# Linear attention with an adapter mixture on one core: one store for a slot, split first loads, values loaded at fixed steps, k passes on ScalarE

## The chip, the cores and the metric

The program runs on one core of a Trainium2 chip. The core has five engines with their own instruction streams, which wait for one another through semaphores: TensorE (PE, with its weight loads shown as PEld), VectorE (DVE), ScalarE (ACT), GpSimd (POOL) and SyncE (SP). SP does no arithmetic here; it issues transfers between HBM and SBUF. Sixteen transfer engines carry them out. The metric is the time of one execution on the device, in microseconds (us); the median of three runs is shown.

## What is computed

An attention with a linear kernel (eight batches, eight heads, 576 positions, 64 features), and behind it a mixture of low-rank adapters of which each row takes two out of eight:

```python
def phi(x, c, s):
    r = np.maximum(x, 0.0)
    return np.concatenate([r * c, r * s], axis=-1)    # c, s: cos, sin of pi/2 * pos/S
q_p = phi(q, cos_w, sin_w)
k_p = phi(k, cos_w, sin_w)
kv = np.einsum('bhsf,bhsd->bhfd', k_p, v)
z = np.sum(k_p, axis=2)
num = np.einsum('bhsf,bhfd->bhsd', q_p, kv)
den = np.einsum('bhsf,bhf->bhs', q_p, z)[..., None] + 1e-06
x = (num / den)                       # then (batch, position) x (head, feature): 4608 x 512
logits = x @ w_gate                   # 8 experts
topk = two largest of logits, w = softmax over these two
out = x + sum over the two of w_k * (x @ A[e]) @ B[e]     # rank 16
```

Inputs and the output are float32; the matrix products run in bf16 with float32 sums.

## The kernel before

**Layout.** A batch's 576 positions are 64 rows of nine neighbours: position 9p + i is row p, column i. Two halves of the heads are stacked, so a tile of k, q or v has 128 partitions (64 rows, twice) and four heads x nine columns x 64 features in each: 1,152 KB in float32. An output tile ("slot", 0 to 35) holds two columns: 128 rows of the output, 64 for each column, 512 values each. Nine slots make a pair of batches; the fifth slot of a pair takes its second column from the second batch.

**Per batch.** `load_k`, `load_q` (SP's queue) and `load_v` (POOL's queue, which also turns v into bf16) bring a batch in. `scale_k(u)` makes relu(k) times cos and sin for one column u of one batch, `kv(u)` multiplies it with v and adds up in PSUM over nine columns, with a column of ones for z. `kv_out` copies the sum to SBUF.

**Per slot n.** `scale_q` (POOL) multiplies two columns of q by cos and sin, four instructions for a slot; `transp_q` (PE) turns them, `evac_q` (DVE) copies them out with the relu; `numden` (PE) makes numerator and denominator; `normalise` (DVE: reciprocal and product) gives the row block xt; `transp_x` (PE) and `evac_x` (DVE) turn it; `logits` (PE) makes x A and x w_gate in one product. Gates are made for groups of three slots (the last slots are groups of two and one): `gate_max`, `gate_a`, `gate_sig` (ACT's sigmoid), `gate_em`, `gate_b`, then `transp_z` and `evac_z` (zgT). `delta` (PE) adds x and z B in PSUM, `evac_o` (ACT, or DVE) copies the sum to SBUF, `store` writes it out.

**Order.** The order on each engine is written out by hand; no scheduler moves anything. The loop runs over n from 0 to 34. In step n the kernel normalises slot n, makes `numden` for n + 1, turns q for n + 2 and scales q for n + 3. `kv_at[n]` lists the columns of k that enter kv in step n; their `scale_k` stands one step earlier. In step n, `age` holds how many steps ago a group's last slot was normalised: at 1 comes `gate_max`, at 2 sigmoid, `gate_em`, `gate_b` and `transp_z`, at 3 `evac_z`; from then on one `delta`, `evac_o` and `store` in each step. Slot d is stored in step d + 5. Behind the loop the last six slots are written out one by one.

**Waits that matter here.** The tile `xz` is one PSUM bank that holds the turned x (columns 0 to 511), the turned z (512 to 895) and a zero that the DVE form of the sin pass reads (line 153). Waits are kept for the tile as a whole: `transp_x` waits for a sin pass on DVE that stands before it, and for `evac_z`. SP and POOL issue in order. Each transfer of SP uses one of eight semaphores in turn and waits until the transfer eight issues earlier has landed. A result tile has 14 buffers (`p_o`), a scaled column of k eight (`p_kp`), v four.

**Start.** SP issues k, v, q of batch 0, k, q of batch 1, then A, w_gate and B, then k, q of batch 2. 32 matmuls on zeros warm PE up. v of batch 0 comes in float32 and is turned into bf16 by DVE and POOL; POOL issues v of batch 1 and 2 before the loop, 3 and 4 in steps 0 and 1 (`load_at`), together with k and q.

Of the kernel before, what the change touches and what calls it, by code (L numbers as in the profile page):

```python
# [18 lines left out]
HALF = 64  # L19
NC = 9  # L20
# [5 lines left out]
def kernel(ctx, tc, q, k, v, w_gate, A, Bw, out):  # L26
# [15 lines left out]
    p_q = ctx.enter_context(tc.tile_pool(name="p_q", bufs=4))  # L42
    p_kp = ctx.enter_context(tc.tile_pool(name="p_kp", bufs=8))
    p_qp = ctx.enter_context(tc.tile_pool(name="p_qp", bufs=3))
# [17 lines left out]

    def part(dram, b):

        a = dram[b, 0:1, 0:1, 0:1]
        return bass.AP(a.tensor, a.offset, [[NC * D, 128], [2 * S * D, HP], [1, NC * D]])

    def load_k(b):
        k_t[b] = p_k.tile([128, HP, NC, D], FP32, name="ks")
        nc.sync.dma_start(out=k_t[b].rearrange("p j i d -> p j (i d)"), in_=part(k, b))  # L70

    def load_q(b):
        q_t[b] = p_q.tile([128, HP, NC, D], FP32, name="qs")
        nc.sync.dma_start(out=q_t[b].rearrange("p j i d -> p j (i d)"), in_=part(q, b))  # L74

# [4 lines left out]

    load_k(0)
    v0 = p_k.tile([128, HP, NC, D], FP32, name="ks")
    nc.sync.dma_start(out=v0.rearrange("p j i d -> p j (i d)"), in_=part(v, 0))
    load_q(0)
    load_k(1)
    load_q(1)

# [41 lines left out]
    Ball = persist.tile([128, DM], BF16, name="Ball")  # L129
    load_k(2)  # L130
    load_q(2)

# [9 lines left out]
    def scale_k(u):  # L142

        b, i = divmod(u, NC)
        kp_t[u] = kp = p_kp.tile([128, HP, 2, D], BF16, name="kp")
        src = k_t[b][:, :, i, :]
        nc.scalar.activation(kp[:, :, 0, :], src, AF.Relu, bias=0.0, scale=cos_tab[:, i:i + 1])  # L147
        if b == 0:
            nc.vector.tensor_scalar(out=kp[:, :, 1, :], in0=src, scalar1=sin_tab[:, i:i + 1],
                                    scalar2=0.0, op0=ALU.mult, op1=ALU.max)  # L150
        elif i % 4 == 3 or (b == 1 and i % 2):

            nc.vector.scalar_tensor_tensor(out=kp[:, :, 1, :], in0=src,  # L153
                                           scalar=sin_tab[:, i:i + 1],
                                           in1=zero.to_broadcast([128, HP, D]),
                                           op0=ALU.mult, op1=ALU.max)
        else:
            nc.scalar.activation(kp[:, :, 1, :], src, AF.Relu, bias=0.0,  # L158
                                 scale=sin_tab[:, i:i + 1])
# [90 lines left out]
    for g, tiles in enumerate(groups):  # L250
        for n in tiles:
            free = groups[g - 1][-1] + 3 if 0 < g < len(groups) - 1 else 0
            due.setdefault(max(n + 1, free, 3), []).append(n)

    def logits(n):
        g = group_of[n]
        i = n - groups[g][0]
        if i == 0:
            za_t[g] = ps.tile([128, 3, ZW], FP32, name="za",
                              tag="qpTp" if g == len(groups) - 1 else "za")  # L260
        xT = xT_t.pop(n)
# [5 lines left out]

    far = set(range(len(groups) - 2))

    def gate_max(g):  # L270
        G = len(groups[g])
        l = za_t[g][:, 0:G, ER:ZW]
        if g in far:
            src = l
            l = p_g.tile([128, 3, 8], FP32, name="lg")
            nc.vector.tensor_scalar(out=l[:, 0:G], in0=src, scalar1=2.0, scalar2=None,
                                    op0=ALU.mult)
            l = l[:, 0:G]
        m8 = p_g.tile([128, 3, 8], FP32, name="m8")
        for i in range(G):  # L280
# [3 lines left out]
                                in1=m8[:, 0:G, 1].to_broadcast([128, G, 8]), op=ALU.is_ge)  # L284
        g_t[g] = (l, m8, mask)

    def gate_a(g):
        G = len(groups[g])
        l, m8, mask = g_t[g]
        nm = p_g.tile([128, 3], FP32, name="nm")  # L290
        t = p_g.tile([128, 3, 8], FP32, name="tg")
        if g in far:
            nc.gpsimd.tensor_tensor(out=nm[:, 0:G], in0=m8[:, 0:G, 0], in1=m8[:, 0:G, 1],  # L293
                                    op=ALU.add)
            nc.gpsimd.tensor_tensor(out=t[:, 0:G], in0=l,
                                    in1=nm[:, 0:G].to_broadcast([128, G, 8]), op=ALU.subtract)
        else:
            nc.vector.scalar_tensor_tensor(out=nm[:, 0:G], in0=m8[:, 0:G, 0], scalar=-1.0,
                                           in1=m8[:, 0:G, 1], op0=ALU.mult, op1=ALU.subtract)
            nc.vector.scalar_tensor_tensor(out=t[:, 0:G], in0=l, scalar=2.0,  # L300
                                           in1=nm[:, 0:G].to_broadcast([128, G, 8]),
                                           op0=ALU.mult, op1=ALU.add)
        g_t[g] = (t, mask)
# [8 lines left out]
    def gate_em(g):  # L312
        G = len(groups[g])
        u, mask = g_t[g]
        em = p_g.tile([128, 3, 8], FP32, name="em")
        eng = nc.gpsimd if g in far else nc.vector
        eng.tensor_tensor(out=em[:, 0:G], in0=u[:, 0:G], in1=mask[:, 0:G], op=ALU.mult)  # L317
        g_t[g] = em
# [15 lines left out]

    def evac_z(g):
        G = len(groups[g])
        zgT_t[g] = t = p_g.tile([128, 3, 128], BF16, name="zgT")
        nc.vector.tensor_copy(t[:, 0:G], xz[:, 512:512 + G * 128].rearrange(
            "p (c s) -> p c s", c=G))

# [10 lines left out]

    def evac_o(n, eng="act"):
        src = osb_t[n]
        osb_t[n] = t = p_o.tile([128, DM], FP32, name="osb")
        if eng == "act":
            nc.scalar.copy(t, src)  # L356
        else:
            nc.vector.tensor_copy(t, src)

    def store(n):  # L360
        t = osb_t.pop(n)
        for pr, (b, i) in zip((lo, hi), columns(n)):
            rows = out[b * S:(b + 1) * S, :].rearrange("(p i) d -> p i d", i=NC)[:, i, :]
            nc.sync.dma_start(out=rows, in_=t[pr, :])

    kv_at = {1: range(9, 13), 2: range(13, 18)}
    u = 2 * NC  # L370
    for b in range(2, B):
        n0 = NS * (b // 2) - 6 if b % 2 == 0 else NS * (b // 2) - 1
        for n, cnt in enumerate((2, 2, 2, 2, 1) if b % 2 == 0 else (3, 2, 2, 2)):
            kv_at[n0 + n] = range(u, u + cnt)
            u += cnt
    load_at = {0: 3, 1: 4, 5: 5, 10: 6, 14: 7}

# [3 lines left out]

    for u in range(NC - 1):
        scale_k(u)
    half = (slice(0, 5), slice(5, NC))
    v0b = v_bufs[0][:, 0:VL].rearrange("p (j i d) -> p j i d", j=HP, i=NC)
    nc.vector.tensor_copy(v0b[:, :, half[0], :], v0[:, :, half[0], :])
    nc.gpsimd.tensor_copy(v0b[:, :, half[1], :], v0[:, :, half[1], :])
    load_v(1)
    for u in range(NC):
        kv(u)  # L390
        if u == 0:
            scale_k(NC - 1)
    scale_q(0, 0)
# [3 lines left out]
    kv_out(0)  # L397
    scale_q(1, 0)
    scale_q(1, 1)
    scale_q(2, 0)  # L400
    scale_q(2, 1)
    load_v(2)
    transp_q(1)
# [3 lines left out]
    for n in range(NT - 1):  # L407
# [3 lines left out]
        normalise(n)  # L411
        for i, u in enumerate(kv_at.get(n + 1, ())):
            scale_k(u)
            if i == 0 and 2 in age:
                gate_sig(age[2])
        if n + 1 not in kv_at and 2 in age:
            gate_sig(age[2])
        if 2 in age:
            gate_em(age[2])
        if n + 3 < NT:  # L420
# [9 lines left out]
        if 1 in age:  # L430
            gate_max(age[1])
            gate_a(age[1])
        if 2 in age:
            gate_b(age[2])
        if 3 in age:
            evac_z(age[3])
            todo += groups[age[3]]
        for u in kv_at.get(n, ()):
# [10 lines left out]
        if n == 2:  # L449
            nc.vector.tensor_copy(AW[:, :, 0:ER].rearrange("p c (e r) -> p e c r", e=E), AWf)  # L450
            nc.vector.tensor_copy(AW[:, :, ER:ZW], Gf)
            nc.vector.tensor_copy(Ball, Bf)
        if n in load_at:
            b = load_at[n]
            load_k(b)
            load_v(b)
            load_q(b)

# [3 lines left out]
    assert not todo and groups[ga:] == [[n - 5, n - 4, n - 3], [n - 2, n - 1], [n]]  # L462
    kv_banks = ps.tile([128, 2, DM], FP32, name="dx_kvz", tag="kvz")
    for t in groups[gb]:
        logits(t)
    normalise(n)
    evac_z(ga)
    transp_x(n)
    gate_max(gb)
    delta(n - 5)  # L470
    evac_o(n - 5)
    store(n - 5)
    evac_x(n)
    logits(n)
    nd_banks = ps.tile([128, 2, DM], FP32, name="dx_nd", tag="nd")
    gate_a(gb)
    gate_sig(gb)
    delta(n - 4, kv_banks[:, 0])
    evac_o(n - 4)
    store(n - 4)  # L480
    gate_max(gc)
    gate_a(gc)
    gate_sig(gc)
    delta(n - 3, kv_banks[:, 1])
    evac_o(n - 3)
    store(n - 3)
    gate_em(gb)
    gate_b(gb)
    transp_z(gb)
    gate_em(gc)  # L490
    gate_b(gc)
    evac_z(gb)
    transp_z(gc)
    delta(n - 2, nd_banks[:, 0])
    delta(n - 1, nd_banks[:, 1])
    evac_o(n - 2)
    evac_z(gc)
    delta(n)
    evac_o(n - 1, "dve")
    evac_o(n)  # L500
    for d in (n - 2, n - 1, n):
        store(d)
# [30 lines left out]
```

## Time and profile before

The runs took 140.83, 140.98 and 141.08 us; the profiled execution took 141.3 us, with a span of 139.5 us from its first to its last instruction and a mean granted TensorE clock of 0.932.

| | before |
|---|---|
| median of the runs | 140.98 us |
| profiled execution, its span | 141.3 us, 139.5 us |
| PE, PEld busy | 104.3 us (75%), 78.1 us (56%) |
| DVE busy | 96.0 us (69%) |
| ACT busy | 76.8 us (55%) |
| POOL busy | 80.0 us (57%) |
| packets, bytes moved | 19,780, 34.44 MB |
| k loads: number, size, median from issue to landing | 8, 1,152 KB, 11.1 us |
| q loads | 8, 1,152 KB, 14.6 us |
| v loads on POOL's queue (bf16 written) | 7, 576 KB, 11.4 us |
| stores | 72, 128 KB, 2.4 us |

How to read the lines of the profile below: a line of slices has 40 digits, one for each fortieth of the span, in tenths busy (9 is 90% or more); DMA is the mean over the 16 transfer engines. A queue's line gives packets, MB and the time that its packets took as a share of 16 engines' span. A line of the chain gives start, duration, and the engine, tile and line of the instruction (SPq: SP's queue). A line of waits reads "engine line <- what it waited for: us in all, times, longest". A line of the timeline gives start, duration, engine, line, operation, tiles and count.

### The profile page before, as it was taken

The numbers are of one execution on the slowest core, as the hardware profiler recorded it, in microseconds if no ns is written. First come the engines' busy times: TensorE is split into PE (matmuls) and PEld (weight loads), VectorE is DVE, ScalarE is ACT, GpSimd is POOL, SyncE is SP. The second block draws the span as 40 slices with busy tenths as digits, with TensorE's granted clock in tenths as the row PEclk, the third lists the DMA queues.
The fourth block names the chain that finished last, engine by engine and source line by source line (L and its number), as shares of the span: only waits on it lengthen the run. The fifth ranks groups of instructions, "written<-read, shape, count | busy, mean of one in ns | idle before, by whom it ended". The sixth has DMA issues, their size and how long they took to land.

```text
span 139.5 us, 4277 instructions
## 1 busy us (share of the span) xinstructions
PE 104.3 (75%) x1665; PEld 78.1 (56%) x1685; DVE 96.0 (69%) x279; ACT 76.8 (55%) x180; POOL 80.0 (57%) x191
## 2 busy tenths in 40 slices
PE   4999469800498978899789598996968899878600
PEld 1347458600487747677477485884747676745200
DVE  3163587141469869889597888968968899998510
ACT  7371781000691386977837967977396934233420
POOL 2038999600079459399495957839658497810000
PEclk9999955995559999999999999999999999999997
DMA  4999999999999999999999999536153344555784
GB/s 93 409 392 393 330 263 267 293 282 294 298 385 404 354 277 377 407 254 189 386 402 298 321 403 353 137 82 138 34 136 80 78 95 112 117 126 128 172 204 108
DMA packets 19780, 34.44 MB, mean 247 GB/s; under 512 B 2736, under 2 KB 6320, under 8 KB 19760
## 3 DMA queue, kind: packets, MB, share of 16 engines
q1 hardware_dynamic: 16064, 30.04, 65.9%
q0 software_dynamic: 3696, 4.13, 17.9%
q8 instruction: 13, 0.21, 0.6%
q14 instruction: 7, 0.06, 0.1%
HBM read 28.85 MB, written 9.44 MB: 274 GB/s over the span
## 4 chain that ended last, share of the span: by engine, by line
PE 31%; DVE 23%; DMA 13%; SPq 12%; ACT 8%; issue 6%; POOL 2%; ACTq 0%; DVEq 0%; POOLq 0%
DMA ks<-in_k_dram 13%; PE qpTp L203 7%; DVE xt L230 6%; SPq L125 5%; PE xz L237 5%; PE za L263 5%; PE nd L221 4%; DVE kp L153 4%; DVE qpT L208 4%; PE kvz L175 4%; ACT kp L147 3%; ACT kp L158 3%; DVE zg L324 3%; DVE xT L242 2%; SPq L74 2%
## 5 line engine op out<-in xcount | busy, mean ns | idle before, releaser
L147 ACT ACTIVATE kp<-ks,cos_tab 128x256 bf16<-128x256 f32 x72 | 34.7, 501 | 20.8 <-DMA ks<-in_k_dram 13.8
L356 ACT COPY osb<-dx 128x512 f32<-128x512 f32 x32 | 18.7, 585 | 29.9 <-PE qpTp L203 16.5
L193 POOL TENSOR_SCALAR qp<-qs,cos_tab 128x256 bf16<-128x256 f32 x71 | 33.9, 478 | 0.8 <-DMA qs<-in_q_dram 0.5
L193 POOL TENSOR_SCALAR qp<-qs,sin_tab 128x256 bf16<-128x256 f32 x71 | 33.8, 475 | 0.0
L237 PE MATMUL xz<-ident,xt 128*128 128x128 bf16 x144 | 15.0, 230 | 20.0 <-DVE kp L153 17.9
L237 PEld LDWEIGHTS <-xt 128*128 128x128 bf16 x144 | 11.6, 117 | 26.9 <-DVE xt L230 15.3
L230 DVE TENSOR_TENSOR xt<-nd,rden 128x512 bf16<-128x512 f32 x36 | 24.9, 691 | 1.2
L208 DVE TENSOR_SCALAR qpT<-qpTp 128x1024 bf16<-128x1024 bf16 x36 | 24.6, 682 | 1.0 <-PE qpTp L203 0.9
L203 PE MATMUL qpTp<-ident,qp 128*128 128x128 bf16 x288 | 23.3, 227 | 0.8 <-POOL qp L193 0.8
L158 ACT ACTIVATE kp<-ks,sin_tab 128x256 bf16<-128x256 f32 x47 | 23.3, 496 | 0.0
L175 PE MATMUL kvz<-v,kp 64*128 64x128 bf16 x576 | 22.5, 225 | 0.0
L175 PEld LDWEIGHTS <-kp 64*128 64x128 bf16 x576 | 17.2, 98 | 3.6 <-issue 0.8
L242 DVE COPY xT<-xz 128x512 bf16<-128x512 bf16 x36 | 15.1, 420 | 5.6 <-PE xz L237 5.2
L203 PEld LDWEIGHTS <-qp 128*128 128x128 bf16 x288 | 17.7, 101 | 1.2 <-issue 0.8
L221 PE MATMUL nd<-kvsb,qpT 128*128 128x65 bf16 (+1 forms) x320 | 17.1, 199 | 1.6 <-DVE qpT L208 1.5
L293 POOL TENSOR_TENSOR nm<-m 128x3 f32<-128x3 f32 x11 | 2.1, 194 | 23.5 <-DVE m L281 23.4
L221 PEld LDWEIGHTS <-qpT 128*128 128x128 bf16 (+1 forms) x320 | 12.7, 103 | 3.4 <-DVE qpT L208 2.9
L263 PE MATMUL za<-AW,xT 128*128 128x136 bf16 x144 | 13.0, 231 | 0.1
L347 PE MATMUL dx<-xt,ident 128*128 128x512 bf16 x31 | 12.0, 388 | 0.0
L216 PE MATMUL nd<-eps_hi,ones 128*128 128x4 bf16 x72 | 12.0, 173 | 0.0
L324 DVE TENSOR_TENSOR zg<-za,em 128x384 bf16<-128x384 f32 (+2 forms) x13 | 6.8, 526 | 7.4 <-POOL em L317 7.3
L153 DVE SCALAR_TENSOR_TENSOR kp<-ks,sin_tab,xz 128x256 bf16<-128x256 f32 x16 | 7.4, 473 | 4.4 <-DMA ks<-in_k_dram 4.4
(59 smaller groups left out, 107.2 us busy)
## 6 DMA issues: line engine op xcount, KB each, us to landing
ks<-in_k_dram SPq DMA_DIRECT2D x8, 1152.0 KB, 11.1
qs<-in_q_dram SPq DMA_DIRECT2D x8, 1152.0 KB, 14.6
out_dram<-osb SPq DMA_DIRECT2D x72, 128.0 KB, 2.4
v<-in_v_dram POOLq DMA_DIRECT2D x7, 576.0 KB, 11.4
ks<-in_v_dram SPq DMA_DIRECT2D x1, 1152.0 KB, 8.0
AWf<-in_moe_A_dram SPq DMA_DIRECT2D x1, 256.0 KB, 22.5
Bf<-in_moe_B_dram SPq DMA_DIRECT2D x1, 256.0 KB, 14.2
Gf<-in_moe_w_gate_dram SPq DMA_DIRECT2D x1, 16.0 KB, 20.4
```

Source lines behind the costliest of these rows:

```text
L147: nc.scalar.activation(kp[:, :, 0, :], src, AF.Relu, bias=0.0, scale=cos_tab[:, i:i + 1])
L158: nc.scalar.activation(kp[:, :, 1, :], src, AF.Relu, bias=0.0, scale=sin_tab[:, i:i + 1])
L175: nc.tensor.matmul(out=kvz_t[b][:, a, j], lhsT=kp[pr, j], rhs=v_rhs(b, j, i, pr), start=(i == 0 and j == 0), stop=(i == NC - 1 and j == HP ...
L193: (eng or nc.gpsimd).tensor_scalar(out=qp_t[n][:, x, :, t, :], in0=q_t[b][:, :, i, :], scalar1=tab[:, i:i + 1], scalar2=1.0, op0=ALU.mult, ...
L203: nc.tensor.transpose(out=t[:, j, :, x, :], in_=qp[:, x, j], identity=ident)
L208: nc.vector.tensor_scalar(out=t, in0=src.rearrange("p j a x s -> p (j a) (x s)"), scalar1=0.0, scalar2=None, op0=ALU.max)
L221: nc.tensor.matmul(out=nd[pr, gg, jj * W:(jj + 1) * W], lhsT=qpT[:, h, pr], rhs=kv_t[b][:, h % 2, h // 2, :], start=False, stop=(jj == 3), ...
L230: nc.vector.tensor_tensor(out=xt, in0=nd[:, :, :, 0:D], in1=rden.rearrange("p (g j) -> p g j", g=2).to_broadcast([128, 2, 4, D]), op=ALU.mult)
L237: nc.tensor.transpose(out=xz[:, c * 128:(c + 1) * 128], in_=xt_t[n][:, c:DM:DCH], identity=ident)
L242: nc.vector.tensor_copy(t, xz[:, 0:512].rearrange("p (c s) -> p c s", c=DCH))
L263: nc.tensor.matmul(out=za_t[g][:, i, :], lhsT=xT[:, c, :], rhs=AW[:, c, :], start=(c == 0 and i == 0), stop=(c == DCH - 1), skip_group_che ...
L356: nc.scalar.copy(t, src)
```

## The change

Six things change; what is computed does not.

- `store` issues one transfer for a slot, with a DRAM side of [2][64][512] in place of two transfers of [64][512].
- The first loads: k, v and q of batch 0 come in two parts by columns (5 + 4, 5 + 4, 4 + 5), k of batch 1 ahead of q's second part; q of batch 1 moves behind A, w_gate and B; k and q of batches 2 and 3 follow there. `scale_k` of batch 0 runs through all nine columns ahead of kv (`p_kp` grows from eight buffers to ten); DVE turns eight columns of v and POOL one.
- v of batch 1 is still loaded before the loop; those of batches 2 to 7 at the ends of steps 3, 6, 9, 13, 17, 21. k and q of batches 4 to 7 are issued at the ends of steps 1, 5, 10 and 14 as before. The columns of batches 2 and 3 enter kv in steps 5 to 7 and 9 to 11, three in each.
- The sin pass of k runs on ACT for all batches from 2 on (before, columns 3 and 7 of each ran on DVE). `evac_z` runs on ACT in the loop. In ACT's order sigmoid and `evac_z` stand ahead of the step's k passes.
- `gate_max` and `gate_a` become one function, always with POOL's two instructions; the last slot has a gate of its own (`gate_last`, `gate_last_em`) with the sigmoid read from PSUM.
- At the end, the last groups' sums and five of the last deltas get PSUM banks of their own, the last result is copied half by ACT and half by DVE, and all six stores stand at the very end of SP's list.

```diff
-    p_kp = ctx.enter_context(tc.tile_pool(name="p_kp", bufs=8))
+    p_kp = ctx.enter_context(tc.tile_pool(name="p_kp", bufs=10))
...
+    def part(dram, b, c0=0, c1=NC):
         a = dram[b, 0:1, 0:1, 0:1]
+        return bass.AP(a.tensor, a.offset + c0 * D,
+                       [[NC * D, 128], [2 * S * D, HP], [1, (c1 - c0) * D]])
+
+    def load(t, dram, b, c0=0, c1=NC):
+        nc.sync.dma_start(out=t.rearrange("p j i d -> p j (i d)")[:, :, c0 * D:c1 * D],
+                          in_=part(dram, b, c0, c1))
...
-    load_k(0)
-    nc.sync.dma_start(out=v0.rearrange("p j i d -> p j (i d)"), in_=part(v, 0))
-    load_q(0)
+    load(k_t[0], k, 0, 0, 5)
+    load(k_t[0], k, 0, 5, NC)
+    load(v0, v, 0, 0, 5)
+    load(v0, v, 0, 5, NC)
+    load(q_t[0], q, 0, 0, 4)
     load_k(1)
-    load_q(1)
+    load(q_t[0], q, 0, 4, NC)
...
-    load_k(2)
-    load_q(2)
+    load_q(1)
+    for b in (2, 3):
+        load_k(b)
+        load_q(b)
...
-        elif i % 4 == 3 or (b == 1 and i % 2):
+        elif b == 1 and i % 2:
...
+    def gate_last(g):
+        l = za_t[g][:, 0, ER:ZW]
+        m8 = p_g.tile([128, 3, 8], FP32, name="m8")
+        nc.vector.max(out=m8[:, 0, :], in_=l)
+        nm = p_g.tile([128, 3], FP32, name="nm")
+        nc.vector.scalar_tensor_tensor(out=nm[:, 0:1], in0=m8[:, 0, 0:1], scalar=-1.0,
+                                       in1=m8[:, 0, 1:2], op0=ALU.mult, op1=ALU.subtract)
+        u = p_g.tile([128, 3, 8], FP32, name="u")
+        nc.scalar.activation(u[:, 0], l, AF.Sigmoid, bias=nm[:, 0:1], scale=2.0)
...
-    def evac_z(g):
+    def evac_z(g, on_act=False):
+        if on_act:
+            nc.scalar.copy(t[:, 0:G], src)
+        else:
+            nc.vector.tensor_copy(t[:, 0:G], src)
...
     def store(n):
-        t = osb_t.pop(n)
-        for pr, (b, i) in zip((lo, hi), columns(n)):
-            rows = out[b * S:(b + 1) * S, :].rearrange("(p i) d -> p i d", i=NC)[:, i, :]
-            nc.sync.dma_start(out=rows, in_=t[pr, :])
+        at = [(b * S + i) * DM for b, i in columns(n)]
+        a = out[0:1, 0:1]
+        rows = bass.AP(a.tensor, a.offset + at[0], [[at[1] - at[0], 2], [NC * DM, HALF], [1, DM]])
+        nc.sync.dma_start(out=rows, in_=osb_t.pop(n))
...
-    kv_at = {1: range(9, 13), 2: range(13, 18)}
-    load_at = {0: 3, 1: 4, 5: 5, 10: 6, 14: 7}
+    kv_at = {1: range(9, 13), 2: range(13, 18), 5: range(18, 21), 6: range(21, 24),
+             7: range(24, 27), 9: range(27, 30), 10: range(30, 33), 11: range(33, 36)}
+    kq_at = {1: 4, 5: 5, 10: 6, 14: 7}
+    v_at = {3: 2, 6: 3, 9: 4, 13: 5, 17: 6, 21: 7}
...
-    nc.vector.tensor_copy(v0b[:, :, half[0], :], v0[:, :, half[0], :])
-    nc.gpsimd.tensor_copy(v0b[:, :, half[1], :], v0[:, :, half[1], :])
+    nc.vector.tensor_copy(v0b[:, :, 0:4, :], v0[:, :, 0:4, :])
+    nc.gpsimd.tensor_copy(v0b[:, :, 4, :], v0[:, :, 4, :])
+    nc.vector.tensor_copy(v0b[:, :, 5:NC, :], v0[:, :, 5:NC, :])
...
         normalise(n)
-        for i, u in enumerate(kv_at.get(n + 1, ())):
+        if 2 in age:
+            gate_sig(age[2])
+            gate_em(age[2])
+        if 3 in age:
+            evac_z(age[3], True)
+            todo += groups[age[3]]
+        for u in kv_at.get(n + 1, ()):
             scale_k(u)
-            if i == 0 and 2 in age:
-                gate_sig(age[2])
...
-        if 3 in age:
-            evac_z(age[3])
-            todo += groups[age[3]]
...
-        if n in load_at:
-            b = load_at[n]
-            load_k(b)
-            load_v(b)
-            load_q(b)
+        if n in v_at:
+            load_v(v_at[n])
+        if n in kq_at:
+            load_k(kq_at[n])
+            load_q(kq_at[n])
...
     n = NT - 1
+    za_bank = ps.tile([128, DM], FP32, name="dx_za", tag="za")
+    delta(n - 4, za_bank)
...
+    evac_o(n, "both")
+    for d in range(n - 5, n + 1):
         store(d)
```

## The prediction

> **What bounds the kernel now.** First the page's slices of 3.49 us and its queues:
>
> ```profile
> PE   4999469800498978899789598996968899878600
> DMA  4999999999999999999999999536153344555784
> q1 hardware_dynamic: 16064, 30.04, 65.9%
> q0 software_dynamic: 3696, 4.13, 17.9%
> ```
>
> The transfer engines are full from 3.5 to 87 us, while PE empties between 28 and 38 us; later they are half idle. Then the chain of waits, in order of time, and the waits by sum:
>
> ```profile
> 18.19 17.89 DMA ks<-in_k_dram
> ...
> 72.46 0.32 PE dx L347
> ...
> 132.84 0.69 DVE osb L358
> ```
> ```profile
> PE xz L237 <- DVE kp L153: 17.9, 12, 9.4
> DVE zg L324 <- POOL em L317: 7.3, 9, 1.2
> ```
>
> Three stretches show. The start ends with the load of k for batch 2, issued at 18.19 and landed at 36.1. The steady loop is a round of DVE and PE: in DVE's timeline the reciprocals of steps 12 and 21 start at 62.29 and 88.39, so nine steps take 26.1 us. The end is SP's own pace:
>
> ```profile
> 125.36 11.23 SPq L364 DMA_DIRECT2D out_dram<-osb  x16
> ```
>
> The last tile is in SBUF at 132.84 + 0.69 = 133.53; SP issues its stores until 136.59, the span ends at 139.5. Last, what a store costs the transfer engines, in a window with stores alone (98.5 to 124), and what a load costs, in one with loads alone (3.4 to 10):
>
> ```profile
> DMA packets 1445, 2.43 MB, mean 95 GB/s; under 512 B 288, under 2 KB 288, under 8 KB 1440
> q1 hardware_dynamic: 1440, 2.36, 40.9%
> ```
> ```profile
> DMA packets 1181, 2.65 MB, mean 401 GB/s; under 512 B 32, under 2 KB 32, under 8 KB 1181
> ```
>
> Of q1's 1,440 packets 288 are short: 18 stores with 64 rows of 2,048 B and 16 short closing packets each, one for every engine. The whole page says the same: 17 loads x 512 + 1,024 + 128 + 128 + 72 x 64 = 14,592 packets of data, and 16,064 - 14,592 = 1,472 = 92 x 16. All 92 transfers of SP's queue were dealt to 16 engines; the outermost count of each, on both sides, is 64 or 128.
>
> **The store, costed first because it decides.** `store` now issues one transfer for a slot in place of two: 36 issues fewer, at the median 0.548 us 19.7 us of SP. But its DRAM side is [2][64][512], its SBUF side 128 rows: the first outermost count in this kernel that 16 doesn't divide. No row of before shows such a transfer, so there are two ends. Near end: dealt to 16 engines as all others. Far end: shares are cut along the outermost count; then there are two, each 64 rows on one engine, and 14 engines get nothing. I take the far end: what the 92 have in common is a count that 16 divides, and 2 is nearest to two shares.
>
> One engine's price of 64 rows, from both sides. Low: 401 GB/s over 16 engines is 25.1 GB/s each, 2,048 B in 81.7 ns, 64 rows in 5.23 us. High: the store window, 0.409 x 16 x 25.5 us / 1,152 = 145 ns, 9.27 us. I take 5.4 (84 ns): in the packet records of before the shortest 2,048 B packets took 82 to 86, those seen when few engines were still writing, and two engines are few.
>
> The Trainium skill speaks against this edit ("DMA: Bandwidth & Descriptors", the section on why a DMA increments its semaphore by 16): the number of engines is the largest up to 16 that divides the slowest dimension's count on both sides. By it the store runs on two engines and the sum is the one below; by the rows of before alone, all on 16, it would be the first rival's. No run here has shown such a store.
>
> **The sum: the work of one such engine.** Its ring is first in, first out, so every load's sixteenth stands between the stores.
> - Until all that is issued ahead of the first store is through: k0 is in use at 6.31, v0 at 9.25, so a load of 1.18 MB takes 2.94 us and the stream starts at 3.3. Eleven loads (k, q of batches 0 to 4, v0) 32.3; the split ones 0.8 more and A, gate and B 2.0 (estimates, from smaller packets); v1 and v2 at 0.179 x 139.5 / 7 = 3.6 us each 7.2. Together 45.6. The first result is stored about then: step 5, which holds its delta, was at 46.5 before.
> - Behind it: k, q of batches 5 to 7, 6 x 2.94 = 17.6; v3 to v7, 5 x 3.6 = 18.0.
> - 36 stores x 5.4 = 194.4 (188.3 by the low price, 333.7 by the high).
> - 45.6 + 17.6 + 18.0 + 194.4 = 275.6. From the last packets (138.0) to the end of the span was 1.5: span 277.1. The profiled execution took 141.3 for a span of 139.5, 1.8 more, and lies 0.3 above the runs' median of 140.98: **278.6** in its terms, **278** for the runs. The two prices give 273 and 418.
>
> Does that engine ever lack work? A result is ready every 2.7 to 2.9 us and a store takes 5.4, so a backlog grows from the first on. SP issues in order with eight transfers under way at most (each issue waits for the semaphore of the eighth before it). k6 and q6 stand behind store 5, k7 and q7 behind store 9: with store 0 and k5, q5 (11.3), five stores (27) and v3, v4 (7.2), k6 lands near 45.6 + 45.5 + 2.9 = 94; with q6, four stores (21.6) and v5, v6, k7 lands near 129; ACT, which scales k, stops in steps 20 and 25 for them. Behind it stop PE's kv, and all after it; but ten stores, 54 us, are queued then. Later the 14 `p_o` buffers set the pace: `evac_o(d)` waits until store d-14 has landed. So the stores run gaplessly.
>
> **The other parts, all under that cover.** If the cover is gone, they make the time of the first rival:
> - Loads. k0, v0 and q0 come in parts, k1 ahead of q0's second, q1 behind A, gate and B; v2 to v4 leave the start. k2 then lands after 3.3 + 6 x 2.94 + 0.8 + 2.0 + 3.6 = 27.3 in place of 36.1: up to 8.8 gained. kv(0) starts at 11.8 behind the warm-up matmuls in any case, so the split alone gains nothing; q0's second part shares with v1 and comes near 19, which delays tile 2 by some 1.6, hidden as far as q1 (near 24.5) is later.
> - v at fixed steps. v2 is issued by POOL behind `gate_max`'s successors of step 3, near 31, and a v takes 11.4 to land (page, median): 42.4. Its first kv is in step 5, which could stand near 35: PE waits 7 us, and `delta`, `transp_x` and DVE behind it. Before, that place was at 45.75: 3.3 of the 8.8 are left, less about 1.5 for a half-speed clock after such a wait (granted 0.76 from 36.2 to 48 before). v3, issued in step 6, waits again for 0 to 4. At step 10 the two kernels are level within 2.
> - Steady loop, nine steps. DVE loses four sin passes and three zgT copies at 0.39 each, 2.7, and the wait for em, 2.8, as the sigmoid now stands ahead of the k passes. In return `transp_x` of each third step waits for ACT, where zgT stands behind a result's evacuation: 0.41 + 0.48 + 0.49 (estimate between 0.585 for 512 and 0.213 for 24 columns) - 0.22 = 1.15 of idle PE, three times 3.5; and once in nine steps six k passes (0.40) and kvsb (0.48) stand ahead of it, 1.3. ACT rises to 2.5 a step, PE needs 2.35. 26.1 becomes 25.5 to 27.5: no gain.
> - End. One issue for a slot, own banks for five deltas, the last tile's gate without POOL, its copy halved between ACT and DVE: the last row of SBUF at 6.5 after the last reciprocal's start for 7.2 before, SP free at once for its two last issues: 2.6 less.
>
> **Rivals.**
> 1. The store is still dealt to 16 engines (closing packets 16 for each). Then it goes faster or level: 141.0 - 2.6 + 0.6 (start and steady) = 139, between 132 (v lands in the least seen, 7.5 us) and 146. For: 92 of 92 did so. Against: their counts all divide by 16. This one lies on the other side; it decides only if all 16 engines close each store.
> 2. Two engines, but a packet costs what it did in the quiet window: 418. Against: there 16 engines drew on 64 rows at once.
> 3. Dealt to 16, and v is late at every batch, not two only (11.4 us against three steps of 2.7): three more waits of 3: 148.
>
> **How the numbers follow.** Forecast 0.84, rivals 0.09, 0.03 and 0.04. 0.2% is about what the measurement tells from no change. Faster: 0.08 of the first rival's 0.09, and 0.01 same; slower 0.91. Time 278. Range: down to 258, where the last loads' 17.6 overlap the stores' time; up to 318, a packet of 101 ns, a third of the way to the high price. The rivals stay outside with less than 2 in 10.
>
> **What would show it.** q1 with 20 x 512 + 1,280 + 4,608 + 23 x 16 + 36 x 2 = 16,568 packets (17,072 with 16 closings); stores landing in tens of us; DMA slices at 1 or 2 tenths with some 50 GB/s from about 60 us on; ACT idle before osb, ended by out_dram; PE, DVE, POOL busy as before in sum. Wrong: stores landing in 2 to 3 us, or an end below 150.

## The result and the profile after

The changed kernel took 271.19 us, median of four runs (270.91 to 271.30), beside 141.03 us for the kernel before in the same session: a ratio of 1.921, 95% interval 1.913 to 1.928. The profiled execution has a span of 269.4 us and a mean granted TensorE clock of 0.715. In the tables further down a time is the median without the executions that took over 1.5% longer than the fastest of their kernel, and ratios go by the same ones; where this changes a median, that of all executions stands in brackets.

From the page of the changed kernel, the slices (6.74 us each now) of PE and of the transfer engines, what these moved (GB/s), and the two queues:

```profile
PE   7938825848986945860088863330000000000000
DMA  7999996893163856128111111111111111111110
GB/s 227 368 272 389 392 318 227 291 222 66 54 124 74 240 202 116 50 61 348 52 53 55 51 54 51 51 51 51 53 51 51 51 51 51 51 51 51 51 51 37
q1 hardware_dynamic: 16568, 30.03, 30.9%
q0 software_dynamic: 3696, 4.13, 9.6%
```

PE has finished by slice 30 of 40; for the last 72 us nothing runs but stores. One tenth of sixteen engines at 51 GB/s is two engines at 25.6. SP's queue holds 16,568 packets, the number that two closing packets for a store give. The waits by sum, then four pieces of the chain of waits (start, duration, what):

```profile
DVE xT L254 <- PE xz L249: 51.4, 23, 16.7
...
PE xz L249 <- ACT zgT L355: 29.7, 11, 16.7
...
ACT osb L374 <- DMA out_dram<-osb: 26.0, 6, 4.5
...
ACT kp L159 <- DMA ks<-in_k_dram: 23.1, 4, 14.5
```
```profile
31.27 12.00 DMA v<-in_v_dram
...
115.21 16.42 DMA ks<-in_k_dram
...
147.11 49.34 DMA out_dram<-osb x3
...
196.93 0.42 DVE osb L379
```

ACT waits for k and for result buffers that are still being written out; PE's largest wait is for ACT, and DVE's largest, for PE, only passes that on. Why k is late can be seen in its packets. Of the load of k of batch 7, issued at 115.21 us, 14 engines sent their closing packets between 124.2 and 124.6; the two that carry the stores were at earlier stores until 128.5 and closed it at 131.3. The last result is in SBUF at 196.93 + 0.42 = 197.35 us. The span ends 72.0 us later, where before it was 6.0 us (133.53 to 139.5). SP, issuing its last twelve stores (timeline: start, duration), shows the pace of the stores:

```profile
193.18 61.71 SPq L386 DMA_DIRECT2D out_dram<-osb  x12
```

The packet records of q1 in that stretch (start us, size, duration ns) show two streams side by side, each with a new packet every 80 ns although each packet takes 84:

```
210.058 2048 84      210.138 2048 84      210.218 2048 84
210.060 2048 84      210.140 2048 84      210.220 2048 84
```

A store is 64 such packets and a closing one on each of two engines, 64 x 80 ns and 6 more: 5.126 us. In the last 23 stores, from 149.99 to 267.88 us, it does not deviate by more than 1 ns.

### The profile page after: what moved, and what is told of

Its sections match the earlier page's. It is cut to its first block, busy times and chain, and to the rows that moved or that the text cites. A ratio compares the mean times of both kernels' runs of the same rounds, so it can differ in the third digit from the quotient of the medians.

```text
span 269.4 us, 4239 instructions
## 1 busy us (share of the span) xinstructions
PE 113.0 (42%) x1665; PEld 86.3 (32%) x1685; DVE 90.2 (33%) x254; ACT 85.9 (32%) x203; POOL 80.4 (30%) x194
## 3 DMA queue, kind: packets, MB, share of 16 engines
q1 hardware_dynamic: 16568, 30.03, 30.9%
## 4 chain that ended last, share of the span: by engine, by line
DMA 39%; PE 19%; ACT 5%; issue 4%; DVE 3%; POOL 2%; SPq 1%; ACTq 0%; POOLq 0%
DMA out_dram<-osb 21%; DMA v<-in_v_dram 9%; DMA ks<-in_k_dram 6%; PE kvz L187 5%; PE qpTp L215 4%; DMA qs<-in_q_dram 3%; PE xz L249 2%; PE nd L233 2%; PE za L275 2%; POOL qp L205 2%; PE dx L366 1%; ACT zgT L355 1%; ACT kp L159 1%; ACT kp L170 1%; PE dx L365 1%
## 5 line engine op out<-in xcount | busy, mean ns | idle before, releaser
L170 ACT ACTIVATE kp<-ks,sin_tab 128x256 bf16<-128x256 f32 x59 | 29.3, 497 | 0.0
L187 PE MATMUL kvz<-v,kp 64*128 64x128 bf16 x576 | 25.0, 243 | 10.1 <-DMA v<-in_v_dram 10.1
L215 PE MATMUL qpTp<-ident,qp 128*128 128x128 bf16 x288 | 25.4, 239 | 2.9 <-POOL qp L205 2.1
L187 PEld LDWEIGHTS <-kp 64*128 64x128 bf16 x576 | 20.0, 108 | 13.7 <-issue 11.3
L233 PE MATMUL nd<-kvsb,qpT 128*128 128x65 bf16 (+1 forms) x320 | 18.4, 206 | 7.0 <-ACT kvsb L192 5.6
L215 PEld LDWEIGHTS <-qp 128*128 128x128 bf16 x288 | 19.4, 108 | 3.7 <-POOL qp L205 2.5
L295 POOL TENSOR_TENSOR nm<-m 128x3 f32<-128x3 f32 (+1 forms) x12 | 2.3, 194 | 47.7 <-DVE m L289 47.7
L365 PE MATMUL dx<-xt,ident 128*128 128x512 bf16 x23 | 9.8, 425 | 3.6 <-ACT osb L374 3.6
L240 DVE RECIPROCAL rden<-nd 128x8 f32<-128x8 f32 x36 | 7.2, 201 | 11.5 <-PE nd L233 11.5
L275 PEld LDWEIGHTS <-xT 128*128 128x128 bf16 x144 | 10.5, 105 | 0.6 <-issue 0.3
## 6 DMA issues: line engine op xcount, KB each, us to landing
v<-in_v_dram POOLq DMA_DIRECT2D x7, 576.0 KB, 10.8
```

The costliest lines, as they stand in the source:

```text
L187: nc.tensor.matmul(out=kvz_t[b][:, a, j], lhsT=kp[pr, j], rhs=v_rhs(b, j, i, pr), start=(i == 0 and j == 0), stop=(i == NC - 1 and j == HP ...
L215: nc.tensor.transpose(out=t[:, j, :, x, :], in_=qp[:, x, j], identity=ident)
L233: nc.tensor.matmul(out=nd[pr, gg, jj * W:(jj + 1) * W], lhsT=qpT[:, h, pr], rhs=kv_t[b][:, h % 2, h // 2, :], start=False, stop=(jj == 3), ...
L275: nc.tensor.matmul(out=za_t[g][:, i, :], lhsT=xT[:, c, :], rhs=AW[:, c, :], start=(c == 0 and i == 0), stop=(c == DCH - 1), skip_group_che ...
```

## The experiments

Each was compared with the kernel before on the same chip, 141.4 to 141.6 us there. Ratios have 95% intervals. Step n below starts where DVE's reciprocal of slot n starts.

### Is it the store alone, and how are engines dealt?

Three kernels. The first is the changed kernel with two stores for a slot, as before:

```diff
-        rows = bass.AP(a.tensor, a.offset + at[0], [[at[1] - at[0], 2], [NC * DM, HALF], [1, DM]])
-        nc.sync.dma_start(out=rows, in_=osb_t.pop(n))
+        for pr, (b, i) in zip((lo, hi), columns(n)):
+            rows = out[b * S:(b + 1) * S, :].rearrange("(p i) d -> p i d", i=NC)[:, i, :]
+            nc.sync.dma_start(out=rows, in_=t[pr, :])
```

> The changed kernel with each slot stored again as two transfers of 64 rows; all its other parts stay. Theory (the one-transfer store was dealt to two engines and that alone set the time): SP's queue shows 16 closing packets for every transfer, stores land in 2 to 5 us, and the time is the first rival's, 139 us (132 to 146). Rival A (v comes late at every batch): 148. Rival B (some other part of the change, not the store, made a good share of the 130 us): above 150.

The second is the kernel before with the new `store` alone.

> The kernel before with the one-transfer store alone. Theory: two engines carry every store and one of them never lacks work; its work is 3.3 + 17 loads x 2.94 + 2.0 + 7 x 3.6 + 36 x 5.126 (64 packets every 80 ns and a closing packet, as the changed kernel's trace has it) + 1.5 = 266.5 us of span, with 0 to 3 us of gaps and 1.8 around the span 268 to 271 us. SP's queue shows 2 closing packets for each store. Rival (other parts of the change made part of the loss): clearly under 260.

The third is the changed kernel with each column stored in two blocks of rows:

```diff
+            for r0, r1 in ((0, 34), (34, HALF)):
+                nc.sync.dma_start(out=rows[r0:r1], in_=t[pr.start + r0:pr.start + r1, :])
```

> The changed kernel with each column stored as two transfers of 34 and of 30 rows, so four transfers for a slot, each an ordinary block of rows. Theory (the number of engines is the largest up to 16 that divides the outermost count): 34 rows go to 2 engines and 30 rows to 15, 17 closing packets for a column, 1,224 for 72 columns; the two busiest engines then carry 2 x (17 + 2) = 38 rows a slot, 36 x 38 x 80 ns = 109 us of stores in place of 184.5, and the time is near 196 us (185 to 202). Rival (what narrows a transfer is the pattern over two columns, and any single block of rows is dealt to all 16): 139 to 146 us, with 16 closing packets for each transfer, 2,304.

| kernel | time | ratio |
|---|---|---|
| changed, two stores a slot | 147.73 us | 1.040 (1.032 to 1.049) |
| before, new store alone | 264.78 us | 1.872 (1.862 to 1.882) |
| changed, blocks of 34 and 30 rows | 195.92 us (one run) | - |

The store alone makes the loss: without it 123 of 130 us are gone, and by itself it brings 123. (264.8 is 3 to 6 us under the 268 to 271 that I had expected; more on its load terms below.) The third decides how. Its queue:

```profile
q1 hardware_dynamic: 17720, 30.04, 44.6%
```

11,520 packets of loads, 4,608 rows and 23 x 16 closings leave 1,224 = 72 x 17: 2 engines for 34 rows, 15 for 30. These are plain blocks of rows, so a pattern over two columns has nothing to do with it; and 38 rows on the busiest engine gave the 196 us worked out from 80 ns a row. That is the rule of the Trainium skill that the prediction weighed ("DMA: Bandwidth & Descriptors", the section on why a DMA increments its semaphore by 16): the largest number up to 16 that divides the slowest count on both sides. The three counts tried here, 2, 34 and 30, agree with it, and so does the 64 of the next group.

But the first kernel lies at 147.7, not at the 139 of my first rival. Its waits, and the place on PE's timeline where the longest begins to end (in brackets: idle before it, and what ended that):

```profile
PE xz L249 <- ACT zgT L355: 12.2, 11, 2.2
...
PE kvz L187 <- DMA v<-in_v_dram: 8.0, 2, 5.5
```
```profile
43.48 0.40 PE L187 MATMUL kvz<-v,kp 64*128 64x128 bf16 x4 [5.53 <-DMA v<-in_v_dram]
```

Step 6 starts 8.3 us earlier than before the change, step 7 only 0.7 earlier, step 12 is 4.6 later, step 35 is 6.6 later. So there are two losses: v in the start, and something in every nine steps.

### v and the zgT copy

From here on the version with two stores a slot is the base. One kernel moves v, one the copy, one makes the store a single transfer in another way, one has the first and the third edit.

```diff
-    v_at = {3: 2, 6: 3, 9: 4, 13: 5, 17: 6, 21: 7}
+    v_at = {0: 2, 3: 3, 6: 4, 10: 5, 15: 6, 20: 7}
```

> The kernel with two stores a slot (147.73 us), with v of batches 2 to 7 issued at the ends of steps 0, 3, 6, 10, 15, 20 in place of 3, 6, 9, 13, 17, 21. Theory (it is slower than before because v of batches 2 and 3 are issued late: step 7 starts 7.6 us after it could, steps 11 and 12 another 5 together, half-speed clock behind the waits included): PE no longer waits for v, step 7 starts near 40 in place of 47.4, and the time is 137 us (134 to 141). Rival (the transfer engines are full there, so v earlier only makes k and q later): 144 to 148, with waits of ACT for k or of POOL for q in the place of PE's for v.

```diff
-        if 3 in age:
-            evac_z(age[3], True)
-            todo += groups[age[3]]
         for u in kv_at.get(n + 1, ()):
...
             gate_b(age[2])
+        if 3 in age:
+            evac_z(age[3])
+            todo += groups[age[3]]
```

> The kernel with two stores a slot (147.73 us), with the zgT copy in the loop back on DVE behind the gate product, as before the change; the sigmoid stays ahead of the k passes and all k passes stay on ACT. Theory (zgT on ACT makes transp_x wait, 1.15 us three times in nine steps and 1.3 more once, against 3 x 0.39 us saved on DVE): nine steps of the steady loop take 24.5 to 26 us in place of 27.0 and 26.8, the time is 144.5 us (142.5 to 146). Rival (the round of DVE and PE sets the loop, so the copies cost there what they save elsewhere): 147 to 149.

The single store with an outermost count of 64 needs neighbouring rows of the output on neighbouring partitions. The products of `delta` can deliver that without an instruction more in the loop: the identity is replaced by a permutation.

```diff
+    nc.vector.tensor_copy(perm.rearrange("p (s x) -> p x s", x=2),
+                          ident.rearrange("p (x s) -> p x s", x=2))
...
-                                identity=ident)                # transp_z
+                                identity=order(groups[g][i]))  # perm, or ident for a mixed slot
...
-        nc.tensor.matmul(out=dx, lhsT=ident, rhs=xt_t.pop(n), start=True, stop=False)
+        nc.tensor.matmul(out=dx, lhsT=order(n), rhs=xt_t.pop(n), start=True, stop=False)
...
+        if b == b1:
+            rows = out[b * S:(b + 1) * S, :].rearrange("(p i) d -> p i d", i=NC)[:, i:i + 2, :]
+            nc.sync.dma_start(out=rows, in_=t)
+            return
```

> The kernel with two stores a slot (147.73 us), with one transfer for each of the 32 slots whose two columns are of one batch, but with the rows of the slot interleaved (a permuted identity in delta and transp_z), so that the outermost count is 64 on the DRAM side and 128 in SBUF; the four mixed slots keep two transfers. Theory (it is the outermost count that deals, not the joining of two transfers): 16 closing packets for each transfer, SP's queue has 17,648 - 32 x 16 = 17,136 packets, SP has 7 issues in place of 12 for the last six slots, so the last store is issued at once when its copy is done, 2.5 us earlier: 145.2 us (144 to 146.5). Rival (a joined store is dealt to few engines whatever its order): above 190. Second rival (the end is set by the landing of the last store, which carries twice the bytes): 147 to 148.

> Both of these edits together: v issued at the ends of steps 0, 3, 6, 10, 15, 20, and one transfer for a slot with interleaved rows. If both theories hold and the gains add: 137 - 2.5 = 134.5 us (131 to 139), so faster than the kernel before. If v earlier only makes k and q later: 142 to 146.

| kernel | time | ratio |
|---|---|---|
| v early | 136.24 us | 0.964 (0.958 to 0.970) |
| zgT on DVE | 140.72 us | 0.994 (0.990 to 0.997) |
| one store, count 64 | 147.65 us (148.04) | 1.046 (1.040 to 1.052) |
| v early, one store, count 64 | 134.42 us (135.17) | 0.954 (0.946 to 0.961) |

**v early: 11.5 us.** Step 7 starts at 38.0 in place of 47.4; no wait of PE for v is left. The packets of v of batches 2, 3 and 4 now run from 27.2 to 50.0 beside the loads of k and q, with the transfer engines at 9 tenths all through. With v late they were at one tenth from 43.8 to 47.5 us: SP issued nothing between 28.1 and 46.5. So v needed only an earlier place among the other loads, and the k and q loads that it pushed back had time to spare (ACT waits 2.9 us for k in place of 1.4, POOL 6.3 for q in place of 6.9). The rival is out.

**zgT on DVE: 7.0 us, more than I expected.** The reciprocals of steps 12, 21 and 30 in DVE's timeline, first with the copy on ACT, then on DVE:

```profile
66.86 0.21 DVE L240 RECIPROCAL rden<-nd 128x8 f32<-128x8 f32 x1 [0.27 <-PE nd L233]
...
93.87 0.21 DVE L240 RECIPROCAL rden<-nd 128x8 f32<-128x8 f32 x1 [0.27 <-PE nd L233]
...
120.67 0.21 DVE L240 RECIPROCAL rden<-nd 128x8 f32<-128x8 f32 x1 [0.27 <-PE nd L233]
```
```profile
66.50 0.21 DVE L240 RECIPROCAL rden<-nd 128x8 f32<-128x8 f32 x1
...
90.41 0.21 DVE L240 RECIPROCAL rden<-nd 128x8 f32<-128x8 f32 x1
...
114.09 0.21 DVE L240 RECIPROCAL rden<-nd 128x8 f32<-128x8 f32 x1
```

Nine steps: 27.0 and 26.8 against 23.9 and 23.7; before the change 26.1. All four of these stretches ran at a granted clock of 1.00. In the other versions with the copy on ACT (v early, one store, both) nine steps took 26.8 to 28.5 us; those of 28.2 to 28.5 had a mean granted clock of 0.94. The same copy, by its tile's view (duration in ns: least, median, most):

```profile
L355 ACT COPY zgT<-xz x11: 477/484/485, 34.6 to 133.7; 128x384 bf16<-128x384 bf16 x11
```
```profile
L357 DVE COPY zgT<-xz x12: 226/346/348, 35.6 to 130.6; 128x384 bf16<-128x384 bf16 x10, 128x256 bf16<-128x256 bf16 x1, 128x128 bf16<-128x128 bf16 x1
```

On ACT it takes 0.14 longer, which is 0.4 in nine steps; the waits put most of the 3.1 down to its place: it stands behind a result's copy (and six k passes in the steps where kv changes batch), and `transp_x` waits for it, 12.2 us in 11 waits. That PE waits for ACT three times in nine steps was right in the prediction (3.5 + 1.3 us); the loop without it is faster than before the change, so some of the other moves pay.

**One store with count 64.** The queue and the issues (KB each, median us to landing) of the single-store version:

```profile
q1 hardware_dynamic: 17136, 30.04, 57.9%
...
out_dram<-osb SPq DMA_DIRECT2D x32, 256.0 KB, 2.6
```

17,136 packets: 16 closings each, and 256 KB land in 2.6 us. Joining two transfers is not what hurt. The end, from the last reciprocal to the end of the span, shrank from 13.0 us to 10.9 (10.8 beside v early). In the time I missed it: 147.65 where 144 to 146.5 was expected. That is in the second rival's window, but the rival's reason, a later landing, does not fit with 2.6 us and the shorter end. The profiled execution, the longest of its four (151.15), waited 12.5 us for v in place of 8.0, and the four executions with two stores themselves lie between 145.81 and 147.99; where the gain went in the executions without a trace is not shown. With v early the store's gain is 1.8 us between medians, with intervals that overlap, and both edits together came as worked out, 134.4 for 134.5.

### All three, and the parts that are left

> The version with v issued early and one interleaved store a slot (135.17 us), with zgT in the loop back on DVE as well. If the loop's gain that the zgT copy alone gave (nine steps 23.8 us in place of 26.9) also holds here, steps 12 to 35 are about 7.5 us shorter and the time is 127.7 us (126 to 131). Rival (the loads of batches 5 to 7 are now what the loop waits for, the transfer engines being full up to 89 us): 131 to 135, with waits for k, q or v in place of the gain.

> The kernel before with one change only: the interleaved single store for the 32 slots whose columns are of one batch, which goes to 16 engines. Theory (one store for a slot is worth what SP's pace costs at the end, 5 issues for the last six slots and nothing earlier): 1.5 to 2.5 us, 139.3 us (138.5 to 140). Rival (72 issues in place of 40 held SP up all along): under 138. Second rival (nothing, as the larger last store lands later): 141.

The next has k of batch 1 one place later:

```diff
     load(q_t[0], q, 0, 0, 4)
-    load_k(1)
     load(q_t[0], q, 0, 4, NC)
+    load_k(1)
```

> The version with all three edits, with the second part of q of batch 0 ahead of k of batch 1 in SP's queue in place of behind it. Theory (behind k it delays tile 2 by some 1.6 us: step 2 starts at 23.7 in place of 22.4 before the change): step 2 starts 1 to 1.6 us earlier, of which 0 to 1 reaches the end, as q of batch 1 sets step 3 to 4. Rival: k of batch 1 comes 1.3 us later and kv in step 1 waits as long: no difference, within 0.5 us.

```diff
-        elif b == 1 and i % 2:
+        elif i % 4 == 3 or (b == 1 and i % 2):
```

> The version with all three edits (126.52 us), with the sin pass of k for columns 3 and 7 back on DVE, as before the change; the sigmoid stays ahead of the k passes. In the two traces nine steps take 26.1 us before the change and 23.9 here. Theory A (moving the sin pass to ACT brought this): nine steps take 25 to 26 us and the time is 130 us (128.5 to 132). Theory B (the sigmoid ahead of the k passes brought it): 23.9 to 24.5 us, 126.5 us (125 to 128).

> The changed kernel with its one-transfer store left as it is, but with the two edits that made the version with two stores a slot 7 and 11 us faster: v issued at the ends of steps 0, 3, 6, 10, 15, 20 and zgT on DVE. Theory (the work of one transfer engine sets the time and covers everything else): 268 to 272 us, as the changed kernel's 271.2, less at most the 2.0 us in which its queue stood empty at 46 us. Rival (the stores' time stands behind the compute, so an earlier start brings an earlier end): 255 to 262.

| kernel | time | ratio |
|---|---|---|
| v early, one store (64), zgT on DVE | 124.36 us (126.52) | 0.879 (0.873 to 0.884) |
| before, one store (64) alone | 139.60 us | 0.986 (0.981 to 0.990) |
| all three, q0 ahead of k1 | 125.01 us | 0.885 (0.881 to 0.890) |
| all three, sin of columns 3, 7 on DVE | 126.49 us (128.09) | 0.895 (0.889 to 0.900) |
| changed kernel, v early, zgT on DVE | 266.51 us | 1.884 (1.872 to 1.895) |

**All three** beat both kernels, by 12% the one before. PE's and the transfer engines' slices of it (3.05 us each):

```profile
PE   3999722898689889899898999989989999877720
DMA  3999999999999999999999999999982352232575
```

PE no longer stands still in the start, where two slices at two tenths are left, and the transfer engines are full without a break until the last load; steps 12 to 21 take 23.9 us. The rival (loads too late for the faster loop) did not come. Of the 17.5 us by which the span is shorter than before the change (122.0 for 139.5), 10.6 are gained by step 12, 4.6 from there to step 35 and 2.3 behind it. The time lies below the expected 126 to 131: the move of zgT also brought step 12 forward, to 51.65 from the 54.15 us of the version without it.

**One store in the kernel before** gives 2.0 us, inside the expectation. Step 35 starts at 126.34 us (126.36 without it) and the end is 1.7 shorter: what SP's pace cost at the end, and no more.

**q0 ahead of k1** is undecided in time: 125.01 against 124.36 us, with intervals of the ratios that overlap. The theory is out all the same. Step 1 starts 2.5 us later, since the first k passes wait for k (4.5 us on ACT) and `transp_x` for one of them on DVE (3.9), and step 2 starts no earlier: at 23.73 against 23.39.

**The sin pass** lies between the theories: back on DVE it costs 2.1 us (126.49 against 124.36, and the intervals of the ratios don't overlap), where one said 3.5 and the other nothing. That 126.49 falls into the second one's window says little, as the window was laid around 126.52. The trace is of an execution of 129.82 us, whose step 12 comes 4.6 us later than in all three (56.22 for 51.65), for a reason that is not shown. From there on its granted clock is 1.00, as in all three, and nine steps take 24.7 and 24.4 us. If that holds for the other executions, the sin pass is 0.7 to 0.8 of the 2.2 us by which the loop is shorter than before the change. The rest, some 1.4, would stay with the sigmoid ahead of the k passes and what goes with it; that order alone was not tried.

**The cover.** In the changed kernel the two edits that are worth 7 and 11.5 us elsewhere bring 4.7 us. That is neither window: 1.5 below the theory's, 4.5 above the rival's upper end. 2.0 of the 4.7 is the stretch at 45.7 us in which no packet was under way, which is gone; the other 2.7 lie in the time that loads and v took beside the stores, and were not resolved further.

## Why the prediction was right, and where it was not

**The deal: right.** Of the two ends I took the far one, and the far one held: two engines, 16,568 packets to the last one, DMA at one tenth with 51 GB/s. The loss was of the size worked out: 277.1 us of span, against 269.4 measured.

**The term that was mis-sized is the store's price.** I took 5.4 us, 64 x 84 ns, from the shortest packet records. 84 ns is a packet's duration; the engine starts the next after 80. 36 x 5.126 = 184.5 in place of 194.4, so 9.9 too much. I had even set 81.7 ns as the low end, from loads; the true step lies below it. The other terms: the load stream in front ended at 45.7 (45.6 worked out); then 2.0 us in which nothing was queued, which I had left out; then 220.2 us, of which 220.2 - 184.5 = 35.7 are the loads in between (17.6 + 18.0 = 35.6 worked out); and 1.5 at the end. 277.1 + 0.1 + 2.0 - 9.9 + 0.1 = 269.4. That the load terms fit so well is partly luck: by the same sum, with no stretch without packets, the two other kernels with this store came out 3.6 us lower (the store alone, 262.9 of span for 266.5) and 2.4 lower (v early and zgT on DVE, 264.9 for 267.3). The share of a load of k on one of the two engines took 2.87 us, where I had 2.94; the rest of that difference was not traced. The low end of the range, 258, is also 3 us below what its reason gives, 278.6 - 17.6 = 261.

**The stops.** k of batch 7 was put at 129 and landed at 131.6, k of batch 6 at 94 and was in use at 101.8; ACT stopped 6.7 and 14.5 us for them, at the first k passes in steps 20 and 25, as worked out. PE then stopped not at kv but one place earlier, for kvsb (5.6 us) and for zgT (16.7), which stand on ACT behind those passes. v of batch 2 was issued at 31.27 and landed at 43.3 (31 and 42.4). "The engine never lacks work" held in so far as from the first store to the last, 47.66 to 267.88, there is no moment without a packet under way.

**The first rival would have been wrong had the store gone to 16 engines.** This was tried: 147.7 us where I worked out 139 (132 to 146). The step that failed is the start: "level within 2 at step 10" held (0.4 ahead), but v of batch 3, which I let wait "0 to 4" without a place in the sum, then makes PE wait 2.4, 3.4 and 5.6 us in three versions (two stores, zgT on DVE, one store of count 64); the granted clock behind the first of these is 0.50 (59 to 62 us), and with two stores a slot step 12 is 4.6 us late. The loop then gave 27.0 with two stores a slot, inside my 25.5 to 27.5, yet 0.8 over the 26.1 on each nine steps, some 2 us by step 35; in the traced execution of the one store of count 64 it gave 28.5 and 28.2, outside. And the end gave 2.2 of the 2.6 (13.1 to 10.9). The third rival's 148 is met in number but not in kind: v waits at two batches, as I had argued against it, not at each.

**"No gain" of the loop** was right for the loop as it stood, but hid that one of its moves cost 3.1 us in nine steps and the rest gained 2.2.

## What to carry to other kernels

Before joining transfers, look at the outermost count on both sides: 64 rows as one block ran on 16 engines, two blocks of 64 in one transfer on two, and the same 128 rows interleaved so that 64 comes first again on 16. A bundle of changes can hold one part that costs everything and others that are worth having: with the store repaired, v earlier and one copy moved back, the same bundle was 12% faster than the kernel before. And a packet's duration is not its price: take the step from one start to the next.

## What the runs showed of the hardware

- Each of the two engines that wrote stores started a 2,048-byte packet every 80 ns (25.6 GB/s), each lasting 84, so packets overlap a little. In the store window of the kernel before, with 16 engines on one block of 64 rows, the share worked out to 145 ns a packet.
- Closing packets count the engines of a transfer: 2 for an outermost count of 2, 17 (2 + 15) for the pair of 34 and 30, 16 for 64.
- A v load on POOL's queue, issued at 31.27 us while the transfer engines stood at 9 tenths, had its first packet at 35.47 and landed at 43.3: a third of its 12 us passed before anything moved.
